# One transpose on TensorE becomes two half-width matmuls, a copy on ScalarE goes, and four masks change engine

## The chip, the cores and the metric

One core of one Trainium2 chip. The metric is the device time of one execution in microseconds. The engines are named as in the profile: PE is TensorE's matmuls and PEld its weight loads, DVE is VectorE, ACT is ScalarE, POOL is GpSimd, SP is SyncE, which here only issues transfers. The kernel before takes 735.45 us (median of 3 runs, 735.43 to 735.67).

## The reference

Attention that keeps only the 32 largest scores of a row, then a gated sum of four two-layer networks (experts), then a layer with the largest of three products:

```
scores = (q @ k^T) / sqrt(64)            # 2 batches, 8 heads, 576 rows, 64 wide, fp32
kth    = 32nd largest score of the row
attn   = exp(scores - max) where scores >= kth, else 0
attn   = attn / (sum(attn) + 1e-9)
x      = attn @ v                        # heads side by side: 1152 x 512
p      = domain_probs / (sum + 1e-9)
out    = sum over e of p[:, e] * (relu(x @ w1[e]) @ w2[e])     # 4 experts, 512 -> 1024 -> 512
h      = max(out @ m1, out @ m2, out @ m3)                     # 512 -> 768
return h @ m_out                                               # 1152 x 512
```

## The kernel before

**Pairs.** The 1152 rows are nine tiles of 128. For attention the heads go two by two, so there are 36 pairs (one tile, two heads), numbered 0 to 35. The tile in the middle (MIXED) holds rows of both batches. Pairs 0 to 3 are tile 0, 4 to 7 tile 1 and so on; 16 to 23 alternate between tiles 4 and 5. Pairs 17, 24, 28 and 32 are the first pairs of tiles 5 to 8: their scores are made early in the kernel, stored to DRAM and loaded back (`later_scores`).

**What a pair does.** `scores` multiplies q and k on PE (pss), ACT copies the result out (s). `topk` finds the 32 largest on DVE in seven steps of eight. `negate` and `exp` prepare and make p = exp(s - max) on ACT. `mask` sets p to zero where s is under the 32nd value and sums it. There are three ways: on DVE in one instruction (line 541), on POOL (lines 544, 545, 549), or on ACT (lines 534 to 536), where no separate exp is made: a Prelu that is steep on one side, a small bias and an Exp with the sum. `ON_ACT` says which pairs do the first and the second head on ACT. `trans_p` transposes p on PE (psp) in pieces of 128 columns, ACT copies them out (pt). `pv` multiplies with v on PE (psv): one full-width matmul (line 601), then eight matmuls (line 604) that alternate between the output partitions 0 to 63 (first head) and 64 to 127 (second head).

**The reciprocal row.** psv holds the unnormalised result with head dimensions on the partitions and the tile's rows along the columns, so the sums, which stand one per partition, must be laid along the columns. `guard` adds 1e-9 on ACT, `recip` makes rr, 128 x 2, on DVE, `spread` copies each of the two numbers to 64 columns on ACT (rb, line 582), `trans_r` transposes that on PE (psr, line 587), ACT copies it out (r, line 589). `norm` multiplies psv by r on DVE, `split_x` makes a high part on ACT and a low part on POOL.

**Products.** Experts and the last layer multiply in three passes of high and low parts: lines 764 to 766. The weights are loaded by SP, rounded to a high part by ACT (whi, line 269), and the low part is the difference, made by POOL or DVE (wlo, line 275).

**Order.** All engines execute in the order in which the program is written. The function `attention` runs over slots, eight per pair, and puts each step of a pair into a slot by a table of numbers (`FIRST`, `MIDDLE`, `TIGHT`, `SECOND`, `THIRD`, `BOTH`, `LOOSE`). A pair whose second head is masked on ACT takes `BOTH`, one masked on DVE takes `LOOSE` (for the later pairs). After each slot, product work is placed until its planned PE time (`clock["pe"]`) has caught up with the planned DVE time (`clock["dve"]`). So the numbers of the table and the DVE work that a step declares set how attention and products alternate on PE. The conversion of the last layer's weights (`to_float32`) starts at slot 306.

Of the kernel before, what the change touches and what calls it, by code (L numbers as in the profile page):

```python
# [10 lines left out]
F32 = mybir.dt.float32  # L11
# [3 lines left out]
AF = mybir.ActivationFunctionType  # L15
# [16 lines left out]
ON_POOL = ((0, 1), (0, 1, 4))  # L32
W_AHEAD = 4
WIDE, W_FROM, W_STEP = 4, 306, 2
ON_ACT = (range(2, 36), (2, 5, 6, 8, 9, 10, 12, 13, 14))
STEEP = 2.0 ** 100
MASK_LATE = 2

FIRST = dict(stag=2, new=1, scores=-12, trans=11, pv=17, rec=16, lag=2, sum=4, late=1)
MIDDLE = dict(stag=2, new=1, scores=-12, at=(11, 12), pv=14, rec=12, lag=1, sum=0, late=1)  # L40
TIGHT = dict(stag=3, new=1, scores=-7, at=(10, 11), guard=11, rec=11, spread=12, pv=12, turn=12, norm=13, split=13, last=14, lag=0, lag_s=1, sum=0, late=1)
SECOND = dict(TIGHT, norm=14, split=14, last=15)
THIRD = dict(stag=4, new=1, scores=-4, at=(11, 12), guard=12, rec=13, spread=13, pv=14, turn=14, norm=15, split=15, last=16, lag=0, lag_s=2, sum=0)
BOTH = dict(stag=4, new=1, scores=-4, at=(14, 14), pv=17, rec=15, lag=2, lag_t=1, sum=0, late=1)
LOOSE = dict(stag=4, new=1, scores=-4, at=(14, 14), pv=17, rec=15, split=22, last=24, lag=2, sum=0)

# [15 lines left out]
def kernel(  # L62
# [14 lines left out]
    nc = tc.nc  # L77
    B, HP, D, _, S = k.shape
    NT, DM = out.shape
    E = gates.shape[2]  # L80
    P = 128
# [13 lines left out]
    def batches(t):  # L95
        return (0, 1) if t == MIXED else (0 if t < MIXED else 1,)
# [16 lines left out]
    at = ctx.enter_context(tc.tile_pool(name="at", bufs=2))  # L113
# [7 lines left out]
    ident = const.tile([P, P], F32, name="ident")  # L121
# [12 lines left out]
    def pe(n):  # L134
        clock["pe"] += n / 2400.0

    def bank(name):
        return pg.tile([P, 512], F32, tag="g", name=name)
# [306 lines left out]
    class Pair:  # L445
        def __init__(self, n):
# [8 lines left out]
            self.on_pool = [n in ON_POOL[j] for j in range(2)]  # L455
            self.on_act = [n in ON_ACT[j] for j in range(2)]

# [119 lines left out]
            dve(60)  # L577
            nc.vector.reciprocal(out=self.rr, in_=self.rs)

        def spread(self):  # L580
            self.rb = at.tile([P, 2, D], F32, tag="rb", bufs=1, name="rb")
            nc.scalar.activation(out=self.rb, in_=self.rr.unsqueeze(2).to_broadcast([P, 2, D]), func=AF.Copy)

        def trans_r(self):
            ps = bank("psr")
            pe(260)
            nc.tensor.transpose(ps[:, 0:P], self.rb.rearrange("p a d -> p (a d)"), ident)
            self.r = at.tile([P, P], F32, tag="r", name="r")
            return lambda: [nc.scalar.activation(out=self.r, in_=ps[:, 0:P], func=AF.Copy), self.did.add("r")]

# [36 lines left out]
    def attention():  # L627

        NP = len(pairs)
        prs = {}  # L630
        later, between = {}, {}

        def options(n):
            return TIGHT if n == HP - 1 else SECOND if n == 2 * HP - 1 else MIDDLE if n in (HP - 2, 2 * HP - 3, 2 * HP - 2) else FIRST if n < 2 * HP else THIRD if n == 3 * HP - 1 else BOTH if n in ON_ACT[1] else LOOSE

        def at_slot(s, f, *a):
            later.setdefault(s, []).append((f, a))


        first_use = {}  # L640
        for n, (c, hp, t) in enumerate(pairs):
            for b in batches(t):
                if ("v", b, hp) not in first_use:
                    first_use["v", b, hp] = n
                    at_slot(8 * n + (options(n)["pv"] - 7 if b and hp else 0), load_v, b, hp)
                if t >= FULL:
                    first_use.setdefault(("k", b, hp), n)
            if t >= FULL and (t, hp) not in later_scores:
                first_use.setdefault(("q", c, hp), n)
            elif n and t < FULL:  # L650
                o = options(max(0, n - 2))
                at_slot(max(8 * n + options(n)["scores"] - LOAD_FULL, 8 * (n - 2) + o["scores"] + o["stag"] + 1), load_full, n)
        free = {"k": -99, "q": -99}
        for key, n in first_use.items():
            if key[0] == "v":
                continue
            s0 = 8 * n
            load, split = (load_k, split_k) if key[0] == "k" else (load_q, split_q)
            at = max(s0 + options(n)["scores"] - (SPLIT_K if key[0] == "k" else SPLIT_Q), free[key[0]] + 2)
            if key[0] == "k" and key[1] and key[2]:  # L660

                at = max(at, 8 * pairs.index((MIXED, key[2] - 1, MIXED)) + options(n)["scores"] + options(n)["stag"] + (1 if key[2] == HP - 1 else 4))
            at_slot(max(at - LOAD, free[key[0]] + 1), load, *key[1:])
            at_slot(at, split, *key[1:])
            free[key[0]] = at
        for n, (c, hp, t) in enumerate(pairs):
            s0 = 8 * n
            prs[n] = Pair(n)
            pr = prs[n]
            o = options(n)  # L670

            def two(s, f, *a, lag=o["lag"]):
                at_slot(s, lambda: at_slot(s + lag, f(*a)))
            for j in range(2):
                b0 = s0 + o["stag"] * j
                two(b0 + o["scores"] - SOONER * ((t, hp) in later_scores), pr.scores, j, lag=o.get("lag_s", o["lag"]))
                for i in range(7):
                    if o["new"]:
                        later.setdefault(b0 + i, []).insert(0, (pr.topk, (j, i)))
                    else:  # L680
                        at_slot(b0 + i, pr.topk, j, i)
                at_slot(b0 + 2, pr.negate, j)
                at_slot(b0 + 5, pr.exp, j)
                late = o.get("late", MASK_LATE) * pr.on_act[j]
                two(b0 + 7 + late, pr.mask, j, lag=o["sum"] if n < EARLY else 3)
                two(s0 + o["at"][j] if "at" in o else b0 + o["trans"] + late + (late > 0), pr.trans_p, j, lag=o.get("lag_t", o["lag"]))
            two(s0 + o["at"][1] if "at" in o else s0 + o["stag"] + o["trans"], pr.trans_p, 2, lag=o.get("lag_t", o["lag"]))
            at_slot(s0 + o.get("guard", o["rec"] - 1), pr.guard)
            at_slot(s0 + o["rec"], pr.recip)
            if o is LOOSE:  # L690
                at_slot(s0 + o["rec"], at_slot, s0 + o["rec"] + 1, pr.spread)
            else:
                at_slot(s0 + o.get("spread", o["rec"] + 1), pr.spread)
            at_slot(s0 + o["pv"], pr.pv)
            two(s0 + o.get("turn", o["rec"] + 2), pr.trans_r)
            end = max(o["pv"], o["rec"] + 2) + o["lag"]
            if n == 1:
                at_slot(s0, nc.sync.dma_start, gate, gates)
            if n == HP - 1:
                between.setdefault(s0 + o["norm"], []).append((norm_gates, ()))  # L700
            if "norm" in o:
                between.setdefault(s0 + o["norm"], []).append((pr.norm, ()))
            else:
                at_slot(s0 + end + 1, pr.norm)
            two(s0 + o.get("split", end + 2), pr.split_x)
        at_slot(-5, load_soon)
        two(9, two_soon, 0, lag=1)
        two(13, two_soon, 1, lag=3)
        for i, t in enumerate((7, *SOON_TWO, 6)):
            at_slot(17 + 3 * i, store_soon, t)  # L710
        last = {}
        for n, p in enumerate(pairs):
            o = options(n)
            last[p[0:2]] = 8 * n + o.get("last", max(o["pv"], o["rec"] + 2) + 2 * o["lag"] + 2)
        for n in range(len(alone)):
            at_slot(ALONE_FROM + ALONE_STEP * n, load_alone, n + 1)
        end = max(last.values()) + 1
        s = min(later)
        while s <= end:
            todo = later.pop(s, [])  # L720
            i = 0
            while i < len(todo):
                f, a = todo[i]
                f(*a)
                todo[i + 1:i + 1] = between.pop(s, [])
                todo += later.pop(s, [])
                i += 1
            if s > 8 * NP + 2:
                clock["dve"] += PAUSE
            yield s, [c for c in last if last[c] + (READY if c[1] == HP - 2 else 0) == s]  # L730
            s += 1

        while narrowed[0] < WIDE * len(wide):
            clock["dve"] += PAUSE
            yield s, []
            s += 1


    lag = []
# [435 lines left out]
```

## Time and profile before

| | before |
|---|---|
| median of 3 runs | 735.45 us |
| profiled execution | 734.86 us |
| its span, first to last instruction | 733.0 us |
| PE busy | 715.2 us (98%) |
| PEld busy | 637.1 us (87%) |
| DVE busy | 580.2 us (79%) |
| ACT busy | 504.8 us (69%) |
| POOL busy | 476.7 us (65%) |

Times in rows are microseconds from the span's start unless they are durations. A PE record lasts longer than it holds the engine, since the next one starts while it drains; what a matmul costs is the distance from its start to the next start. Attention ends near 446 us; products run from about 34 us to the end. The timeline merges equal instructions that follow each other into one row with a count.

### The profile page before, as it was taken

The numbers are of one execution on the slowest core, as the hardware profiler recorded it, in microseconds if no ns is written. First come the engines' busy times: TensorE is split into PE (matmuls) and PEld (weight loads), VectorE is DVE, ScalarE is ACT, GpSimd is POOL, SyncE is SP. The second block draws the span as 40 slices with busy tenths as digits, with TensorE's granted clock in tenths as the row PEclk, the third lists the DMA queues.
The fourth block names the chain that finished last, engine by engine and source line by source line (L and its number), as shares of the span: only waits on it lengthen the run. The fifth ranks groups of instructions, "written<-read, shape, count | busy, mean of one in ns | idle before, by whom it ended". The sixth has DMA issues, their size and how long they took to land. (4 is left out here: it accounts for less than half of the span.)

```text
span 733.0 us, 13786 instructions
## 1 busy us (share of the span) xinstructions
PE 715.2 (98%) x4758; PEld 637.1 (87%) x4758; DVE 580.2 (79%) x1174; ACT 504.8 (69%) x1127; POOL 476.7 (65%) x416
## 2 busy tenths in 40 slices
PE   5899999999999999999999999999999999999997
PEld 3687679889999998899988998999889998998996
DVE  7999989989999999999999974766879873323441
ACT  4868889899987886788888876556566753442431
POOL 2514779678989975879779867856745773532520
PEclk9999999999999999999999999999999999999999
DMA  8995555635756553555455436786879855543501
GB/s 238 303 281 203 146 180 156 181 113 165 208 154 197 150 164 111 170 170 177 137 165 173 139 122 216 267 299 209 294 238 338 256 189 211 167 147 114 188 1 43
DMA packets 57813, 135.26 MB, mean 185 GB/s; under 512 B 9936, under 2 KB 23120, under 8 KB 57744
## 3 DMA queue, kind: packets, MB, share of 16 engines
q1 hardware_dynamic: 49248, 125.74, 54.7%
q10 hardware_dynamic: 8496, 8.65, 3.4%
q8 instruction: 37, 0.61, 0.3%
q14 instruction: 32, 0.26, 0.1%
HBM read 123.36 MB, written 11.01 MB: 183 GB/s over the span
## 5 line engine op out<-in xcount | busy, mean ns | idle before, releaser
L275 POOL TENSOR_TENSOR wlo<-raw,whi 128x512 fp32r<-128x512 f32 x252 | 332.0, 1347 | 135.1 <-ACT whi L269 124.8
L269 ACT ACTIVATE whi<-raw 128x1024 fp32r<-128x1024 f32 x164 | 169.9, 1058 | 18.6 <-PE ps L766 10.2
L764 PE MATMUL ps<-xl,whi 128*128 128x256 f32 (+1 forms) x584 | 173.6, 297 | 0.5 <-POOL xl L625 0.5
L766 PE MATMUL ps<-xh,wlo 128*128 128x256 f32 (+1 forms) x584 | 170.7, 292 | 0.0
L765 PE MATMUL ps<-xh,whi 128*128 128x256 f32 (+1 forms) x584 | 170.6, 292 | 0.0
L513 DVE MAX8 m<-work 128x8 f32<-128x576 f32 x216 | 155.1, 744 | 0.1
L764 PEld LDWEIGHTS ps<-xl,whi 128*128 128x128 f32 x584 | 110.8, 190 | 1.6 <-POOL xl L625 0.7
L765 PEld LDWEIGHTS ps<-xh,whi 128*128 128x128 f32 x584 | 109.7, 188 | 0.9 <-issue 0.2
L766 PEld LDWEIGHTS ps<-xh,wlo 128*128 128x128 f32 x584 | 109.7, 188 | 0.0
L515 DVE MATCH_REPLACE8 work<-m,work 128x576 f32<-128x576 f32 x144 | 106.6, 741 | 0.0
L275 DVE TENSOR_TENSOR wlo<-raw,whi 128x1024 fp32r<-128x1024 f32 x38 | 54.7, 1445 | 49.7 <-ACT whi L269 36.8
L764 PE MATMUL ps<-wlo,h 128*128 128x512 f32 x224 | 91.0, 406 | 2.1 <-POOL wlo L275 1.9
L766 PE MATMUL ps<-whi,h 128*128 128x512 f32 x224 | 87.8, 392 | 0.0
L765 PE MATMUL ps<-whi,h 128*128 128x512 f32 x224 | 87.6, 391 | 0.0
L245 POOL TENSOR_TENSOR narrow<-narrow,raw 128x256 int32<-128x256 int32 x48 | 46.5, 976 | 21.3 <-DMA narrow<-narrow 5.7
L513 DVE MAX8 m<-s 128x8 f32<-128x576 f32 x71 | 53.1, 747 | 2.5 <-ACT s L495 2.5
L495 ACT ACTIVATE s<-pss 128x288 f32<-128x288 f32 x128 | 45.5, 401 | 12.0 <-PE pss L475 7.1
L515 DVE MATCH_REPLACE8 work<-m,s 128x576 f32<-128x576 f32 x72 | 53.3, 741 | 0.0
L764 PEld LDWEIGHTS ps<-wlo,h 128*128 128x128 f32 x224 | 42.8, 191 | 11.3 <-POOL wlo L275 5.0
L562 ACT ACTIVATE pt<-psp 128x512 f32<-128x512 f32 x72 | 40.0, 600 | 15.7 <-PE psp L559 15.6
L766 PEld LDWEIGHTS ps<-whi,h 128*128 128x128 f32 x224 | 42.1, 188 | 9.9 <-POOL h L904 0.5
L1042 DVE TENSOR_TENSOR tm<-ps,tm 128x384 f32<-128x384 f32 x36 | 19.8, 556 | 39.0 <-PE ps L766 39.0
(118 smaller groups left out, 1493.7 us busy)
## 6 DMA issues: line engine op xcount, KB each, us to landing
raw<-in_w_dram SPq DMA_DIRECT2D x128, 512.0 KB, 4.3
raw<-narrow SPq DMA_DIRECT2D x36, 512.0 KB, 4.5
raw<-in_m_dram SPq DMA_DIRECT2D x36, 256.0 KB, 5.1
whole<-in_w_dram SPq DMA_DIRECT2D x14, 512.0 KB, 5.5
narrow<-narrow ACTq DMA_DIRECT2D x48, 128.0 KB, 5.0
kraw<-in_k_dram SPq DMA_DIRECT2D x16, 288.0 KB, 4.5
raw<-in_mo_dram SPq DMA_DIRECT2D x12, 256.0 KB, 5.8
kfull<-in_k_dram SPq DMA_DIRECT2D x9, 288.0 KB, 5.2
```

The source lines that it names most:

```text
L245: nc.gpsimd.tensor_tensor(out=out.bitcast(I32), in0=out.bitcast(I32), in1=last, op=ALU.add)
L269: nc.scalar.activation(out=hi, in_=raw, func=AF.Copy)
L275: on.tensor_tensor(out=lo[:, x], in0=raw[:, x], in1=hi[:, x].bitcast(F32), op=ALU.subtract)
L495: nc.scalar.activation(out=s[:, h, :], in_=halves[h][:, 0:SH], func=AF.Copy)
L513: nc.vector.max(m[:, 8 * r:8 * r + 8], src)
L515: nc.vector.match_replace(out=self.w[j], in_to_replace=m[:, 8 * r:8 * r + 8], in_values=src, imm_value=NEG)
L562: return lambda: [nc.scalar.activation(out=d, in_=ps.rearrange("p (r n) -> p r n", r=NR), func=AF.Copy), self.did.add(("pt", part))]
L764: nc.tensor.matmul(ps, lhsT=lh, rhs=rl, start=first, stop=False)
L765: nc.tensor.matmul(ps, lhsT=lh, rhs=rh, start=False, stop=False)
L766: nc.tensor.matmul(ps, lhsT=ll, rhs=rh, start=False, stop=last)
L1042: nc.vector.tensor_tensor(out=tm[:, g], in0=ps, in1=tm[:, g], op=ALU.max)
```

## The change

`spread` goes with its tile rb. `trans_r` makes psr with two matmuls: the weights are one column of rr, read as 64 equal columns, the moving side is the identity, the output 64 partitions each. `trans_r` now stands in the slot of `pv` for all pairs. The pairs 17, 24, 28 and 32 enter the second list of `ON_ACT`, and with it take the table `BOTH` in place of `LOOSE`.

```
-ON_ACT = (range(2, 36), (2, 5, 6, 8, 9, 10, 12, 13, 14))
+ON_ACT = (range(2, 36), (2, 5, 6, 8, 9, 10, 12, 13, 14, 17, 24, 28, 32))
...
-TIGHT = dict(stag=3, new=1, scores=-7, at=(10, 11), guard=11, rec=11, spread=12, pv=12, turn=12, norm=13, split=13, last=14, lag=0, lag_s=1, sum=0, late=1)
+TIGHT = dict(stag=3, new=1, scores=-7, at=(10, 11), guard=11, rec=11, pv=12, norm=13, split=13, last=14, lag=0, lag_s=1, sum=0, late=1)
...
-        def spread(self):
-            self.rb = at.tile([P, 2, D], F32, tag="rb", bufs=1, name="rb")
-            nc.scalar.activation(out=self.rb, in_=self.rr.unsqueeze(2).to_broadcast([P, 2, D]), func=AF.Copy)
-
         def trans_r(self):
             ps = bank("psr")
             pe(260)
-            nc.tensor.transpose(ps[:, 0:P], self.rb.rearrange("p a d -> p (a d)"), ident)
+            for j in range(2):
+                nc.tensor.matmul(ps[j * D:(j + 1) * D, 0:P], lhsT=self.rr[:, j:j + 1].to_broadcast([P, D]), rhs=ident, start=True, stop=True)
...
-            if o is LOOSE:
-                at_slot(s0 + o["rec"], at_slot, s0 + o["rec"] + 1, pr.spread)
-            else:
-                at_slot(s0 + o.get("spread", o["rec"] + 1), pr.spread)
             at_slot(s0 + o["pv"], pr.pv)
-            two(s0 + o.get("turn", o["rec"] + 2), pr.trans_r)
+            two(s0 + o["pv"], pr.trans_r)
```

On PE, at the first pair (its psv, and the pss of later pairs behind it), the rows before:

```order
L601 MATMUL psv<-pt_303,v_last_112 128x128
L604 MATMUL psv<-pt,vt 64x128 x8
L475 MATMUL pss<-kfull,qfull 128x288
L348 MATMUL pss<-kfull,qraw 128x288
L475 MATMUL pss<-kfull,qfull 128x288
L348 MATMUL pss<-kfull,qraw 128x288
L587 MATMUL psr<-ident,rb 128x128
L559 MATMUL psp<-ident,p 128x128 x4
```

and after (line numbers are smaller by 3 or 7 in the new file):

```order
L598 MATMUL psv<-pt_303,v_last_112 128x128
L601 MATMUL psv<-pt,vt 64x128 x8
L584 MATMUL psr<-ident,rr 64x128 x2
L475 MATMUL pss<-kfull,qfull 128x288
L348 MATMUL pss<-kfull,qraw 128x288
L475 MATMUL pss<-kfull,qfull 128x288
L348 MATMUL pss<-kfull,qraw 128x288
L559 MATMUL psp<-ident,p 128x128 x4
```

Here psr has moved ahead of four pss; the fifth pair moves in the same way. At the ninth pair, as in all the rest, psr stood directly behind psv before and still does, with the products behind it. Before:

```order
L601 MATMUL psv<-pt_1442,v_last_112 128x128
L604 MATMUL psv<-pt,vt 64x128 x8
L587 MATMUL psr<-ident,rb 128x128
L764 MATMUL ps_1469<-xl,whi 128x256
L765 MATMUL ps_1469<-xh,whi 128x256
```

and after:

```order
L598 MATMUL psv<-pt_1434,v_last_112 128x128
L601 MATMUL psv<-pt,vt 64x128 x8
L584 MATMUL psr<-ident,rr 64x128 x2
L757 MATMUL ps_1461<-xl,whi 128x256
L758 MATMUL ps_1461<-xh,whi 128x256
```

Nothing else moved there: one row of one instruction is one of two.

On ACT, around the second head of pair 17 (its 32 largest values are m_2812 before and m_2796 after), before:

```order
L495 ACTIVATE s<-pss 128x288 x2
L562 ACTIVATE pt<-psp 128x512 x2
L567 ACTIVATE pt_2856<-psp 128x128
L582 ACTIVATE rb<-rr 128x128
L534 ACTIVATE s<-s,m_2701 128x576
L535 ACTIVATE nb<-m_2701,nb 128x1
L536 ACTIVATE p,rs<-s,nb 128x576
L527 ACTIVATE p<-s,nb 128x576
L413 ACTIVATE qh<-qraw 128x512
L520 ACTIVATE nb<-m_2872 128x1
L495 ACTIVATE s<-pss 128x288 x2
```

and after:

```order
L562 ACTIVATE pt<-psp 128x512 x2
L567 ACTIVATE pt_2840<-psp 128x128
L413 ACTIVATE qh<-qraw 128x512
L520 ACTIVATE nb<-m_2856 128x1
L495 ACTIVATE s<-pss 128x288 x2
L895 ACTIVATE raw<-ps_2729 128x512
L269 ACTIVATE whi<-raw 128x1024 x2
L586 ACTIVATE r<-psr 128x128
L387 ACTIVATE kT<-kraw 128x576 x2
L534 ACTIVATE s<-s,m_2796 128x576
L535 ACTIVATE nb<-m_2796,nb 128x1
L536 ACTIVATE p,rs<-s,nb 128x576
```

The spread (rb) and the exp of line 527 are gone, and the three instructions of the second head's mask stand some ten instructions later, behind the rounding of weights and of k. The mask of the first head (m_2701) stands ahead of the copies pt in the new order. In PE's whole list no matmul is added or lost but for psr; about the four pairs, groups of products and of scores stand somewhat earlier or later.

## Rows read from the trace of the kernel before

**Rows 1.** The page: busy us, share and count by engine; granted clock in slices.

```profile
PE 715.2 (98%) x4758; PEld 637.1 (87%) x4758; DVE 580.2 (79%) x1174; ACT 504.8 (69%) x1127; POOL 476.7 (65%) x416
...
PEclk9999999999999999999999999999999999999999
```

**Rows 2.** Busy us by stretch: length, PE, PEld, DVE, ACT, POOL, clock, DMA, GB/s.

```profile
80.00:446.00 366.00, 362.05 (x2767) 324.29 (x2766) 343.07 (x732) 303.72 (x719) 299.85 (x261) 1.00 0.53 161
446.00:629.00 183.00, 182.78 (x1028) 167.89 (x1027) 127.76 (x230) 105.35 (x196) 112.55 (x97) 1.00 0.73 247
629.00:733.00 104.00, 100.32 (x549) 95.44 (x547) 34.94 (x47) 38.00 (x53) 35.91 (x24) 1.00 0.33 109
```

**Rows 3.** What PE's matmuls waited for: us in total, times, longest.

```profile
PE ps L764 <- POOL wlo L275: 1.9, 5, 0.8
...
PE psp L559 <- ACT p L536: 0.3, 1, 0.3
```

**Rows 4.** Groups by line and shape: count, busy us, mean ns, idle before.

```profile
L534 ACT ACTIVATE s<-s,m 128x576 f32<-128x576 f32 x43 | 33.4, 777 | 0.3 <-DVE m L513 0.3
L536 ACT ACTIVATE p<-s,nb 128x576 f32<-128x576 f32 x43 | 33.4, 777 | 1.4
...
L527 ACT ACTIVATE p<-s,nb 128x576 f32<-128x576 f32 x29 | 22.2, 764 | 0.0
...
L535 ACT ACTIVATE nb<-m,nb 128x1 f32<-128x1 f32 x43 | 12.6, 293 | 0.0
L582 ACT ACTIVATE rb<-rr 128x128 f32<-128x128 f32 x36 | 11.5, 318 | 7.4 <-DVE rr L578 7.3
...
L541 DVE SCALAR_TENSOR_TENSOR p<-s,m,p 128x576 f32<-128x576 f32 x24 | 27.3, 1136 | 5.4 <-ACT p L527 5.4
```

**Rows 5.** What PE's weight loads waited for, same columns as rows 3.

```profile
PEld psp L559 <- ACT p L536: 1.4, 2, 1.1
...
PEld psr L587 <- ACT rb L582: 0.5, 2, 0.3
```

**Rows 6.** Timeline of PE near 47 us: start, length, instruction, count.

```profile
46.78 1.17 PE L850 MATMUL psa<-xfull,whole 128*128 128x128 f32 x9
47.78 0.60 PE L559 MATMUL psp<-ident,p 128*128 128x128 f32 x4
48.22 0.61 PE L850 MATMUL psa<-xfull,whole 128*128 128x128 f32 x4
```

**Rows 7.** Timeline of PE at the ninth pair, two windows, and psv's group.

```profile
115.71 1.09 PE L604 MATMUL psv<-pt,vt 128*64 128x128 f32 x16
116.74 0.33 PE L587 MATMUL psr<-ident,rb 128*128 128x128 f32 x1
...
115.98 0.83 PE L604 MATMUL psv<-pt,vt 128*64 128x128 f32 x12
...
L604 PE MATMUL psv<-pt,vt 128*64 128x128 f32 x512 | 35.0, 279 | 0.0
```

**Rows 8.** Timeline of PE at the fifth and at the third pair.

```profile
68.34 1.09 PE L604 MATMUL psv<-pt,vt 128*64 128x128 f32 x16
69.37 1.24 PE L475 MATMUL pss<-kfull,qfull 64*128 64x288 f32 x4
...
43.58 0.33 PE L587 MATMUL psr<-ident,rb 128*128 128x128 f32 x1
43.84 1.23 PE L475 MATMUL pss<-kfull,qfull 64*128 64x288 f32 x4
```

**Rows 9.** POOL's longest wait, and the timeline of PE around a hole.

```profile
POOL wlo L275 <- ACT whi L269: 124.8, 40, 10.7
...
103.41 0.39 PE L765 MATMUL ps<-whi,h 128*128 128x512 f32 x1
103.64 0.40 PE L766 MATMUL ps<-whi,h 128*128 128x512 f32 x1
104.31 0.50 PE L764 MATMUL ps<-wlo,h 128*128 128x512 f32 x1 [0.28 <-POOL wlo L275]
```

More of the change, by code (lines that the diff above doesn't have):

```diff
@@ L40 @@
 MIDDLE = dict(stag=2, new=1, scores=-12, at=(11, 12), pv=14, rec=12, lag=1, sum=0, late=1)
-TIGHT = dict(stag=3, new=1, scores=-7, at=(10, 11), guard=11, rec=11, spread=12, pv=12, turn=12, norm=13, split=13, last=14, lag=0, lag_s=1, sum=0, late=1)
+TIGHT = dict(stag=3, new=1, scores=-7, at=(10, 11), guard=11, rec=11, pv=12, norm=13, split=13, last=14, lag=0, lag_s=1, sum=0, late=1)
 SECOND = dict(TIGHT, norm=14, split=14, last=15)
-THIRD = dict(stag=4, new=1, scores=-4, at=(11, 12), guard=12, rec=13, spread=13, pv=14, turn=14, norm=15, split=15, last=16, lag=0, lag_s=2, sum=0)
+THIRD = dict(stag=4, new=1, scores=-4, at=(11, 12), guard=12, rec=13, pv=14, norm=15, split=15, last=16, lag=0, lag_s=2, sum=0)
 BOTH = dict(stag=4, new=1, scores=-4, at=(14, 14), pv=17, rec=15, lag=2, lag_t=1, sum=0, late=1)
```

## Prediction

> **What bounds the kernel now.** I read the page first: TensorE (PE) holds matmul records for 715.2 of 733.0 us, 98%, and its granted clock is at full speed in all slices [rows 1]. A busy PE need not be a limiting PE, so the busy times by stretch come next [rows 2]: from 80 us to the end of attention near 446 us PE is busy for 362.05 of 366 us, so it is without work for only 3.95 us. From 446 to 629 us it lacks 0.22 us, and what it lacks after 629 us (3.7 us) is mostly the last output. VectorE (DVE) is close behind in attention (343.07 of 366), ScalarE (ACT) and GpSimd (POOL) are 17 and 18% free there. In the list of what PE waited for, last, the entries behind the weights' low halves and behind a masked p come to 1.9 and 0.3 us [rows 3]. The conclusion is the frame for all that follows: PE executes a fixed list in a fixed order with hardly a hole, so the time moves by what the list gets longer or shorter, plus what is won from or lost in holes. An engine beside PE that gets lighter pays only through the holes.
>
> **The path of the reciprocal row.** Before, per pair: reciprocal on DVE, spread to 128 columns on ACT (rb), one transpose on PE (psr), copy on ACT (r). After: reciprocal, two plain matmuls of 64 output partitions each against the identity, copy. 36 pairs.
>
> What goes from ACT: 36 spreads of 318 ns, 11.5 us, and up to 7.4 us in which ACT stood idle in front of one, mostly for the reciprocal [rows 4]. PE waited for the spread nearly nowhere: the spread is named in 0.5 us of psr's waits of the weight load, which runs beside the matmuls [rows 5]. So the shorter chain is worth 0.5 us at most directly, and nothing at least.
>
> What comes to PE: the price is read from distances between starts, since a record's own duration overlaps its neighbours. A transpose of 128 columns holds PE for 0.11 us: four start at 47.78 and the next work at 48.22 [rows 6]. A plain fp32 matmul of 128 columns over the whole array stands in the trace as two records at 0.11 us each: nine records from 46.78 to 47.78. So two plain matmuls one after the other would be four records, 0.44 us. But they use the two halves of the array's columns, as the psv matmuls of line 604 do. There the eight matmuls are 16 records in 1.09 us, and the last twelve of them 0.83 us from 115.98 on; less one record's own length (their mean is 0.28) these twelve start within 0.55 us, in five steps of two records, 0.11 us a step [rows 7]. One after the other, 16 records would take 1.7 us. So two records, one of each half, run together, and the new pair of matmuls costs two steps, 0.22 us, against 0.11 us: +0.11 us. The weights have one odd feature, one number per partition read 64 times, that no row shows. The bounds per pair are thus +0.0 us (all four records together: the sum does not change) and +0.33 us (no two together: 36 x 0.33 = 11.8 us). I take +0.11, since the psv rows have the same form (128 rows by 64 columns, 128 moving columns, fp32) and stand right in front of the new ones.
>
> Then the switch between forms. The last psv records start at 115.98 + 0.55 = 116.53 and psr at 116.74 [rows 7]; this step, out of the column halves, is 0.2 rather than 0.11 us. Leaving the halves costs the same when a 64-row matmul follows: from the first psv record to pss it is 68.34 to 69.37, 1.03 us, as from 115.71 to 116.74 here [rows 7, 8]. Today that 0.1 us stands between psv and psr; after, the new psr is of psv's form, and the switch comes behind it. It is moved, not removed. Two pairs win a little: where psr is followed by pss of line 475 it costs 0.26 us to the next start (43.58 to 43.84) [rows 8], a second switch into row halves; after, there is one switch, so these two stand at 1.03 + 0.22 = 1.25 instead of 1.03 + 0.26 = 1.29, about -0.05. In two early pairs (the first and the fifth) psr also moves one slot ahead, next to psv; there the switch between pss and the transposes stays, so I count them as all others. Sum on PE: 34 x 0.11 - 2 x 0.05 = 3.6 us. Nothing covers this: PE is the engine with 3.95 us of holes in 366, and the matmuls are in its list at places where it does not wait.
>
> The Trainium skill, "TensorEngine Tiling (Array Packing)", section Key Properties, says that different tiles can run in parallel and that changing the tiling mode drains TensorE. Both sentences agree with the rows: the pairs of psv records, and the 0.1 us on leaving the halves. By the second alone the change would look good, a switch saved per pair; the order shows that psv's own switch remains behind the new matmuls, so it saves none in 34 pairs of 36.
>
> **The four masks.** The pairs 17, 24, 28 and 32 lose their second head's mask on DVE (1136 ns, 4 x 1.14 = 4.5 us) and on ACT the exp (764 ns), and get on ACT 777 + 293 + 777 = 1847 ns, so 4 x 1.08 = 4.3 us more [rows 4]; the short read of the sum behind each, on both engines, is left out. All this is beside PE. ACT ends up lighter in all: -11.5 + 4.3 = -7.2 us. The pairs also take the settings of the other pairs whose two masks are on ACT (lag 1 on the transposes, the split a slot sooner). The planner counts 4 x 0.67 = 2.7 us less DVE work, so it puts that much less product work between attention steps: PE's list keeps all its matmuls, and those move behind attention, where PE is full too. The cost is nothing at either end as work; as waits it lies between minus a share of the holes and the price of a later p, which the rivals hold. In the trace the 43 masks already on ACT make PE wait 0.3 us in all, and its weight load 1.4 us [rows 3, 5].
>
> **The sum.** PE +3.6 us. From the holes I take back the 0.5 us above. +3.1 us on the profiled execution, 734.86 us (span 733.0 and 1.9 around it), gives 738.0. The median of the runs is 735.45, 0.59 above that execution, so the forecast is 735.45 + 3.1 = 738.5 us.
>
> **Rivals.** What a measurement can tell from no change is about 0.2%, 1.5 us.
>
> 1. Faster: ACT's relief ends PE's waits behind the low halves of the weights. The place is PE's line 764 on wlo, which POOL makes from ACT's whi: POOL waited 124.8 us for whi [rows 9]. One such hole: starts 0.23 us apart, then 103.64 to 104.31, so 0.44 us lost where the row shows 0.28 of idle [rows 9]. By that ratio the 3.95 us of holes cost 3.95 x 0.44 / 0.28 = 6.2 us. If all went, 3.6 - 6.2 = -2.6: 732.9 us. It is faster by the bound once 5.1 of 6.2 us are won, while PE names wlo for 1.9 us of its waits at most and the transposed or masked p for others [rows 3]. For it: ACT is lighter by 7.2 us of work and loses up to 7.4 us of idle time in front of the spreads. Against: four pairs put blocks of 1.8 us on ACT, the very thing that stands ahead of whi. 9%.
>
> 2. No measurable difference: a third to four fifths of these 6.2 us are won, or the added PE time falls into holes whose releaser does not follow PE. 735.45 + 3.6 - 3.1 = about 736. 17%.
>
> 3. The two halves do not run together, because the weights are read with a step of zero or two matmuls are too few to overlap: +11.8 us, 747. Against: eight psv matmuls overlap from the first record on. 5%. The Trainium skill, "TensorE: Matmul & The Clock Gate", section Terms, says that transposes have a mode four times faster for FP32; by it one plain matmul would be 4 x 0.11 = 0.44 us, so two in parallel give the same +0.33 and 747 us. The trace has two records against one for the same columns, a factor of two, so I do not raise the chance.
>
> 4. The mask on ACT becomes a wait of PE: p is ready up to 1.85 us after its turn in four pairs, 7.4 us at full exposure, half of it likely if at all: 738.5 + 3.7 = 742.2. Against: the nine pairs that already have both masks there. 8%.
>
> **How the numbers follow.** Forecast +3.1 with its own range +1.5 to +6 (one more hole per block of ACT masks at 0.4 to 0.9 us, or more holes filled): 61%. Faster is rival 1 alone, 0.09; same is rival 2, 0.17; slower is the forecast with rivals 3 and 4, 0.74. The range takes in the forecast and all of rival 2 (down to 735.0) and the lower half of rival 4 (to 742.0); it leaves out rivals 1 and 3 and the rest.
>
> **What would show it.** In the changed profile psr should be 144 records in 36 groups, in steps of two records 0.11 us apart, with psv to the next product start 0.11 us longer; PE's busy time near 719 us; ACT's near 498 (504.8 - 7.2); DVE's near 576 (580.2 - 4.5); PE's holes from 80 us to the end of attention 3 to 5 us. If the four records come one by one, rival 3 is right; if PE's holes fall under 1 us, rival 1; if psp waits for p on ACT at the four pairs, rival 4. The prediction is wrong if psr costs PE no more than the transpose did, or if the time falls while psr costs what I say: then holes were worth more than the trace of before shows.

## The result, and the profile after

The changed kernel takes 739.83 us (median of 6 runs, 739.47 to 740.71) against 735.56 us before on the same chip: ratio 1.0055, 95% interval 1.0042 to 1.0068, so 3.1 to 5.0 us slower (4.05 by the ratio, 4.3 by the medians). The forecast was 738.5 us, +3.1 us.

One thing is needed to read the numbers of single runs. In the profiled execution the granted clock of PE stood at its lower level, 1.2 GHz, from 26.0 to 29.5 us, after PE had been idle 2.0 us for a pt (before: idle 2.1 us at the same place, the clock stayed at 2.4 GHz). PE's timeline there (start, length, instruction, count, idle before it and its releaser):

```profile
26.21 0.79 PE L598 MATMUL psv<-pt,v_last 128*128 128x128 f32 x2 [2.03 <-ACT pt L567]
26.93 1.98 PE L601 MATMUL psv<-pt,vt 128*64 128x128 f32 x16
```

The first psv took 1.98 us instead of 1.09, and the span is 738.4 us instead of 737.4 to 737.7 in the four runs without it. Below, times are compared from the sixth pair on (psr at 76.10 before, 77.23 after): from there to the end it is 656.9 us before and 661.2 us after, +4.3 us.

Page of the changed kernel, busy time by engine, and its busy times by stretch (length, PE, PEld, DVE, ACT, POOL, clock, DMA, GB/s):

```profile
PE 721.3 (98%) x4866; PEld 644.3 (87%) x4866; DVE 578.8 (78%) x1166; ACT 500.1 (68%) x1103; POOL 474.4 (64%) x416
```

```profile
80.00:446.00 366.00, 362.64 (x2827) 326.01 (x2827) 340.38 (x724) 300.37 (x699) 294.16 (x258) 1.00 0.52 158
446.00:629.00 183.00, 182.16 (x1038) 167.38 (x1035) 129.88 (x231) 105.49 (x197) 116.02 (x101) 1.00 0.76 252
```

PE has 108 more records (4866 for 4758): 144 of psr for 36. DVE is lighter by 1.4 us and ACT by 4.7 [rows 1], where the forecast counted 4.5 and 7.2: the four masks took 4.2 us off DVE, but its 38 differences wlo lasted 1495 ns each for 1445, and of the 2.5 us by which ACT differs the short reads of the sums, left out of the count, make 0.7. PE's idle time is 3.36 us up to 446 us and 0.84 us up to 629 us, 4.20 in all, against 3.95 + 0.22 = 4.17 us [rows 2]. So the holes up to 629 us have the same idle time, and the loss stands in the list.

The ninth pair, PE's timeline after, which answers to [rows 7]:

```profile
116.85 1.09 PE L601 MATMUL psv<-pt,vt 128*64 128x128 f32 x16
117.78 0.39 PE L584 MATMUL psr<-ident,rr 128*64 128x128 f32 x4
118.09 0.39 PE L757 MATMUL ps<-xl,whi 128*128 128x256 f32 x1
118.32 0.28 PE L758 MATMUL ps<-xh,whi 128*128 128x256 f32 x1
```

Four records of psr in 0.39 us, two steps, right behind the psv records with no switch between: 0.93 us from the first psv record, not 1.03 [rows 7]. Then come 0.31 us from the first record of psr to the first product and another 0.23 to the second, which in a run of products stands 0.12 behind the first. Before, psr to the first product was 0.08 and on to the second 0.20. From the first psv record to the second product it is 1.47 us, before 1.31 (115.71 to 117.02): +0.16, where the forecast had +0.11. From the record ahead of psv to the second product it is 0.15 to 0.17 us more at the other late pairs too, where PE does not wait and the neighbours are the same kind of work.

What PE waited for, after (total, times, longest):

```profile
PE psv L598 <- ACT pt L567: 4.1, 5, 2.0
...
PE ps L757 <- POOL wlo L275: 1.0, 4, 0.3
PE ps L757 <- DVE h L904: 0.8, 1, 0.8
```

and before, for pt:

```profile
PE psv L601 <- ACT pt L567: 3.1, 3, 2.1
```

The waits behind wlo fell from 1.9 us [rows 3] to 1.0. The three waits for pt that were there before (near 26, 94 and 144 us) are still there and two have come, near 298 and 399 us; the wait for h is new. PE's rows at the longer of the two and at h:

```profile
297.56 0.29 PE L483 MATMUL pss<-kT,qh 128*128 128x288 f32 x1
298.64 0.49 PE L598 MATMUL psv<-pt,v_last 128*128 128x128 f32 x2 [0.78 <-ACT pt L567]
...
469.75 0.34 PE L759 MATMUL ps<-xh,wlo 128*128 128x384 f32 x1
470.93 0.41 PE L757 MATMUL ps<-xl,whi 128*128 128x384 f32 x1 [0.84 <-DVE h L904]
```

### The profile page after: what moved, and what is told of

Same layout as the page of the kernel before. It is cut to its first block, busy times and chain, and to the rows that moved or that the text cites. A ratio compares the mean times of both kernels' runs of the same rounds, so it can differ in the third digit from the quotient of the medians.

```text
span 738.4 us, 13987 instructions
## 1 busy us (share of the span) xinstructions
PE 721.3 (98%) x4866; PEld 644.3 (87%) x4866; DVE 578.8 (78%) x1166; ACT 500.1 (68%) x1103; POOL 474.4 (64%) x416
## 5 line engine op out<-in xcount | busy, mean ns | idle before, releaser
L275 DVE TENSOR_TENSOR wlo<-raw,whi 128x1024 fp32r<-128x1024 f32 x38 | 56.6, 1495 | 56.3 <-ACT whi L269 43.8
```

What stands on the lines that cost most here:

```text
L275: on.tensor_tensor(out=lo[:, x], in0=raw[:, x], in1=hi[:, x].bitcast(F32), op=ALU.subtract)
```

## The experiments

Ten kernels ran in three groups, each group on one chip beside runs of the kernel before (medians 735.27 to 735.88); the ratios are against those. The changed kernel itself ran in none of the groups, so where a kernel is set against it the two times come from different groups.

**1. The reciprocal row alone.**

```
-ON_ACT = (range(2, 36), (2, 5, 6, 8, 9, 10, 12, 13, 14, 17, 24, 28, 32))
+ON_ACT = (range(2, 36), (2, 5, 6, 8, 9, 10, 12, 13, 14))
```

> The new reciprocal row alone (no spread, two half-width matmuls); the masks stay where they were before. Theory A: the matmuls are the whole loss. From the changed kernel's trace, behind the half-width records the next product starts 203 ns later and the one behind that 226 ns later, so a pair costs 0.158 us more on PE than before, about 4.9 us over all pairs; with 0.5 us taken back from holes about 739.9 us, the same as the changed kernel's 739.8 within 1 us. Rival B: the masks carry the loss through new waits (psv for pt, and the product at 470 us); then this kernel is near 736 to 737.

Measured: 740.6 us (739.08 to 741.53), ratio 1.0046 (1.0022 to 1.0070). It is as slow as the whole change: theory A. From the sixth pair to the end its trace is 5.35 us longer than before. Two of PE's waits have come or grown, for h (none before) and for wlo at pso (0.2 us before):

```profile
PE psp L564 <- DVE h L904: 1.6, 1, 1.6
...
PE pso L757 <- DVE wlo L275: 1.2, 1, 1.2
```

**2. The masks alone**, the same line edited in the kernel before.

> The four masks on ScalarE alone; spread and transpose as before. Theory A: 735.5 within 0.7 us, since only VectorE and ScalarE change. Rival B (the masks carry the loss): 738 to 739.5.

Measured: 739.17 us (737.62 to 739.99), ratio 1.0031 (1.0013 to 1.0049). Theory A falls here: the masks are not free. They lose 2.3 us alone by the ratio (3.3 by the medians, 3.05 from the sixth pair on in the traces), the row alone 3.4 (4.7, 5.35) and the whole change 4.05 (4.3, 4.3), so the two parts don't add up. PE's own list is that of the kernel before but for the order; its idle time from 80 to 446 us is 6.6 us (359.40 busy) for 3.95. PE's waits, and its timeline at the largest hole:

```profile
PE psv L601 <- ACT pt L567: 5.3, 5, 1.9
```

```profile
296.45 0.29 PE L483 MATMUL pss<-kT,qh 128*128 128x288 f32 x1
298.29 0.49 PE L601 MATMUL psv<-pt,v_last 128*128 128x128 f32 x2 [1.55 <-ACT pt L567]
```

and ACT there:

```profile
293.44 0.60 ACT L909 ACTIVATE h<-ps 128x512 fp32r<-128x512 f32 x1
295.24 0.78 ACT L534 ACTIVATE s<-s,m 128x576 f32<-128x576 f32 x1 [1.20 <-DVE m L513]
295.93 0.28 ACT L535 ACTIVATE nb<-m,nb 128x1 f32<-128x1 f32 x1
296.24 0.78 ACT L536 ACTIVATE p<-s,nb 128x576 f32<-128x576 f32 x1
296.92 0.19 ACT L536 ACTIVATION_READ_ACCUMULATOR p<-s,nb 128x1 f32 x1
297.01 1.06 ACT L562 ACTIVATE pt<-psp 128x512 f32<-128x512 f32 x2
297.97 0.28 ACT L567 ACTIVATE pt<-psp 128x128 f32<-128x128 f32 x1
```

ACT stands idle 1.20 us for the 32nd value, does a mask, and only then the three copies pt. This is not the mask that moved to ACT but one that was on ACT before; in the new order it stands ahead of pt.

**3. ScalarE relieved, by a wide reciprocal on VectorE** (in the kernel before, `spread` left empty).

```
-            nc.vector.reciprocal(out=self.rr, in_=self.rs)
+            nc.vector.reciprocal(out=self.rb, in_=self.rs.unsqueeze(2).to_broadcast([P, 2, D]))
```

> The kernel before without the spread on ScalarE: the reciprocal on VectorE reads each sum 64 times and writes the 128 columns itself, the transpose stays. It takes the 11.5 us from ScalarE as the change does, adds about 0.12 us per pair to VectorE and nothing to PE. Theory A (ScalarE's relief pays only through PE's holes): 735.0, between 734.3 and 735.6. Rival C (the relief is worth some us and the matmuls ate it): 731 to 733.5.

Measured: 748.3 us (748.06 to 748.95), ratio 1.0153 (1.0123 to 1.0183). Neither theory: the experiment failed by its own cost. VectorE's group of the reciprocal:

```profile
L578 DVE RECIPROCAL rb<-rs 128x128 f32<-128x128 f32 x36 | 33.8, 939 | 0.5 <-ACT rs L572 0.5
```

939 ns, not the 0.27 assumed: 28 us more on VectorE, which is then busy for 360.64 of 366 us, and PE waits at many places.

**4. Which matmul stands behind the switch** (in the changed kernel; psr also goes ahead of psv).

```
-                nc.tensor.matmul(ps[:, cols], lhsT=last, rhs=self.pt[2][:, cols], start=True, stop=False)
                 for r in range(NR):
...
+                nc.tensor.matmul(ps[:, cols], lhsT=last, rhs=self.pt[2][:, cols], start=False, stop=True)
```

> The changed kernel with PE's order turned within psv: psr first, then the eight half-width psv matmuls, then the full-width one of the tail, so that a full-width fp32 matmul and not a product stands behind the switch out of the column halves. Same matmuls in number and size. Theory A: the mis-sized 0.05 us per pair is the switch meeting the product's weights; it goes, 36 x 0.05 = 1.8 to 2 us: 737.8. Rival D (the cost lies in the halves' own steps or anywhere in the switch, wherever it stands): 739.8 within 0.7.

Measured: 738.72 us (738.35 to 741.09), ratio 1.0034 (1.0013 to 1.0055): 1.1 us under the changed kernel by the medians, between the theories; the intervals overlap, so the total decides nothing. The timeline does:

```profile
115.23 0.29 PE L483 MATMUL pss<-kT,qh 128*128 128x288 f32 x1
115.45 0.44 PE L584 MATMUL psr<-ident,rr 128*64 128x128 f32 x4
115.72 1.04 PE L600 MATMUL psv<-pt,vt 128*64 128x128 f32 x16
116.70 0.49 PE L602 MATMUL psv<-pt,v_last 128*128 128x128 f32 x2
116.94 0.36 PE L757 MATMUL ps<-xl,whi 128*128 128x256 f32 x1
117.14 0.28 PE L758 MATMUL ps<-xh,whi 128*128 128x256 f32 x1
```

From the last pss to the second product: 1.91 us. In the changed kernel, from a pss at 116.41 to 118.32: 1.91. Before, 115.27 to 117.02: 1.75. The pair's price did not move, so the switch costs the same before a product and before a plain fp32 matmul (D). What this kernel won came from holes: from the record ahead of the pair to the second one behind it, it takes 2.33 us for 2.92 near 94 us, 2.51 for 2.96 near 297 us and 2.03 for 2.47 near 398 us, all places where psv waits for pt in the changed kernel.

**5. psr twice** (in the changed kernel).

```
-            for j in range(2):
+            for j in (0, 1, 0, 1):
```

> The changed kernel with the two half-width matmuls of psr issued twice (the second two write the same values again). Theory A (PE is the bound and a step of two half-width records costs 0.109 us, as between the new records): 36 x 0.218 = +7.8 us over the changed kernel, 747.4; somewhat less if holes take some of it, at least 746. Rival E (PE has slack in attention that hides added matmuls): under 743.5.

Measured: 747.91 us (747.33 to 749.16), ratio 1.0163 (1.0135 to 1.0190): +8.1 us over the changed kernel, theory A. At the ninth pair:

```profile
118.69 1.09 PE L601 MATMUL psv<-pt,vt 128*64 128x128 f32 x16
119.61 0.61 PE L584 MATMUL psr<-ident,rr 128*64 128x128 f32 x8
120.15 0.38 PE L757 MATMUL ps<-xl,whi 128*128 128x256 f32 x1
120.37 0.28 PE L758 MATMUL ps<-xh,whi 128*128 128x256 f32 x1
```

From psv to the second product 1.68 us, 0.21 more than with two matmuls: 36 x 0.21 = 7.6 us of the 8.1. Work added to PE's list reaches the end in full.

**6. The masks with the old table** (in the kernel with the masks alone).

```
-            return TIGHT if n == HP - 1 else SECOND if n == 2 * HP - 1 else MIDDLE if n in (HP - 2, 2 * HP - 3, 2 * HP - 2) else FIRST if n < 2 * HP else THIRD if n == 3 * HP - 1 else BOTH if n in ON_ACT[1] else LOOSE
+            return TIGHT if n == HP - 1 else SECOND if n == 2 * HP - 1 else MIDDLE if n in (HP - 2, 2 * HP - 3, 2 * HP - 2) else FIRST if n < 2 * HP else THIRD if n == 3 * HP - 1 else BOTH if n in ON_ACT[1] and n < 16 else LOOSE
```

> The four masks on ScalarE alone, as in the run of the masks before, but the four pairs keep the table of the pairs masked on VectorE (LOOSE instead of BOTH). On ScalarE the copies pt then stand ahead of the neighbour's mask again, as in the kernel before. Theory F: the masks' loss of some 3 us is this order: PE's psv waits for a pt that stands behind a mask which waits for VectorE. Then the holes of 1.7 and 1.0 us at psv go and the time is 736 within 0.7. Rival G: the 4.3 us of work on ScalarE, or the planner's smaller product share, is the loss: 738 to 739, like the masks alone.

Measured: 735.52 us (735.09 to 742.30), ratio 1.0002 (0.9976 to 1.0028). Theory F: the same four masks on ACT, the loss gone. ACT and PE at the same place as in the second experiment:

```profile
293.14 0.60 ACT L909 ACTIVATE h<-ps 128x512 fp32r<-128x512 f32 x1
293.62 1.09 ACT L562 ACTIVATE pt<-psp 128x512 f32<-128x512 f32 x2
294.57 0.31 ACT L567 ACTIVATE pt<-psp 128x128 f32<-128x128 f32 x1
295.73 0.31 ACT L582 ACTIVATE rb<-rr 128x128 f32<-128x128 f32 x1 [0.85 <-DVE rr L578]
```

```profile
296.10 0.29 PE L483 MATMUL pss<-kT,qh 128*128 128x288 f32 x1
296.24 0.38 PE L601 MATMUL psv<-pt,v_last 128*128 128x128 f32 x2
```

The copies pt come first, and psv follows pss at once.

**7. The whole change with the old table** (the same edit in the changed kernel).

> The changed kernel, but the four pairs keep LOOSE instead of BOTH. Theory F: the two psv holes of 0.95 and 0.35 us go, so 738.5 to 739.3. Rival G: the same as the changed kernel, 739.8 within 0.5.

Measured: 738.67 us (737.91 to 739.87), ratio 1.0032 (1.0011 to 1.0054), in the range of theory F. Both psv holes are gone from its trace; the 1.0 us one near 468 us stays. So the table costs about 1.2 us in the change by the medians (1.5 from the sixth pair on in the traces; the intervals of the two kernels overlap), where PE is later at psv anyway, and more when the masks move alone.

**8 and 9. ScalarE relieved, by GpSimd and by VectorE** (in the kernel before).

```
-            nc.scalar.activation(out=self.rb, in_=self.rr.unsqueeze(2).to_broadcast([P, 2, D]), func=AF.Copy)
+            nc.gpsimd.tensor_copy(out=self.rb, in_=self.rr.unsqueeze(2).to_broadcast([P, 2, D]))
```

and with `nc.vector.tensor_copy`.

> The kernel before with the spread made by GpSimd instead of ScalarE; transpose and masks as before. ScalarE is relieved of 11.5 us and of the idle time in front, PE has no added work, GpSimd gets 36 copies of about 0.46 us. Theory A (ScalarE's relief pays only through PE's holes): 735.2 between 734.3 and 736. Rival C (the relief is worth some us): 731 to 733.5. If GpSimd's queue delays the transposes, psr waits for rb show it, and the time is over 737.

> The kernel before with the spread made by a copy on VectorE right behind its own point in the order, instead of on ScalarE; transpose and masks as before. ScalarE is relieved as in the change; VectorE, 94% busy in attention, gets 36 copies of some 0.2 to 0.3 us (its 128x128 product takes 0.27), 7 to 10 us. Theory A (VectorE's added work shows only where it makes holes on PE): 735.5 to 738.5. Rival C (ScalarE's relief is worth some us by itself): 731 to 734.

Measured: GpSimd 768.91 us (768.45 to 774.57), ratio 1.0456 (1.0422 to 1.0491); VectorE 739.36 us (738.88 to 739.79), ratio 1.0053 (1.0039 to 1.0068). With GpSimd PE waits in psr:

```profile
PE psr L587 <- POOL rb L582: 26.4, 12, 6.3
```

The copy itself is short (0.29 us) but queues behind GpSimd's other work, mostly the weights' low halves. The granted clock also stood at 1.2 GHz for 17 us in four stretches between 124 and 254 us, each near a wait of PE of 2.2 to 6.3 us, so the 33 us over the kernel before are not all waiting. With VectorE, ACT is lighter by 7.1 us from 80 to 446 us (296.63 for 303.72), yet DVE rises to 356.77 of 366 us and PE's idle time to 7.45 us. Rival C, a gain from a lighter ScalarE, showed in none of the three runs; but each loaded another engine, so a free relief was not measured and this stays open.

Why the copies on VectorE took 18.6 us and not 7 to 10 stands in the rows of both engines. One copy, and GpSimd beside it:

```profile
225.93 1.23 DVE L582 COPY rb<-rr 128x128 f32<-128x128 f32 x1
...
224.25 2.83 POOL L388 TENSOR_TENSOR kT<-kraw,kT 64x576 fp32r<-64x576 f32 x2
227.16 3.79 POOL L275 TENSOR_TENSOR wlo<-raw,whi 128x512 fp32r<-128x512 f32 x3
```

The copy ends 0.08 us after the GpSimd instruction that was running when it started. Of 36 copies, the 11 that started with GpSimd idle took 196 to 227 ns; of the other 25, 24 ended 82 to 89 ns after the GpSimd instruction beside them did.

**10. Toward a kernel under both** (in the sixth kernel).

```
-WIDE, W_FROM, W_STEP = 4, 306, 2
+WIDE, W_FROM, W_STEP = 4, 308, 2
```

> The kernel before with the four masks on ScalarE, the table LOOSE kept for these pairs, and the conversion of the last layer's weights begun two slots later (308 for 306). The one hole left against the kernel before, 1.0 us at 465 us, is a product that waits for VectorE's h, which stands behind a conversion. Theory H: later conversions free VectorE there, the hole goes and the time is 734.5 within 0.7, so at best 0.1 to 0.2% under the kernel before. Rival J: the hole or another one comes back elsewhere, above all where the conversion ends near 617 us: 735.5 to 737.5.

Measured: 734.71 us (733.60 to 739.29), ratio 0.9994 (0.9978 to 1.0010). PE lacks nothing from 446 to 629 us in its trace, so the hole went as theory H says; its gain over the kernel before cannot be told from none.

```profile
446.00:629.00 183.00, 183.00 (x1030) 168.42 (x1029) 128.42 (x229) 105.29 (x195) 110.38 (x98) 1.00 0.75 249
```

## Why the prediction was right, and where it was off

**The frame was right.** PE executes a list with few holes, and what is added to the list is added to the time: doubling psr gave 8.1 us for 7.6 counted, and the row alone was as slow as the whole.

**The price of psr: right in kind, small by a third.** The forecast's step "the new pair of matmuls costs two steps, 0.22 us, against 0.11 us: +0.11 us" is exact for the steps: 144 records, psr 0.93 us behind the first psv and two steps of 0.11. "It is moved, not removed" is where it was mis-sized: the forecast took the 0.1 us up to the next start for the whole switch. Leaving the halves costs 0.2 us in all (0.31 - 0.22 = 0.09 to the first product, 0.23 - 0.12 = 0.11 more to the second). Before, it cost 0.15: 0.10 ahead of psr, and 0.05 behind it, since psr to the second product took 0.28 where 0.11 + 0.12 would do. The transpose behind the halves had hidden the other 0.05. The 0.20 from the first product to the second is by itself no mark of the switch; before, it stands behind transposes with no halves near as well, where the two steps together are 0.23:

```profile
111.93 0.27 PE L564 MATMUL psp<-ident,p 128*128 128x128 f32 x1
111.96 0.36 PE L764 MATMUL ps<-xl,whi 128*128 128x256 f32 x1
112.16 0.28 PE L765 MATMUL ps<-xh,whi 128*128 128x256 f32 x1
```

The fourth kernel shows that the cost is not that of a product behind the switch: a plain fp32 matmul there changed nothing. So a pair costs 0.16. Why a transpose hides a part, no run shows. The two pairs before a 64-row pss were right: psv to pss took 1.24 us (43.76 to 45.00) where 1.25 was worked out:

```profile
43.76 1.09 PE L601 MATMUL psv<-pt,vt 128*64 128x128 f32 x16
...
45.00 0.51 PE L475 MATMUL pss<-kfull,qfull 64*128 64x288 f32 x1
```

With 0.16 for 0.11 the forecast's sum over 36 pairs becomes 5.3 us, not 3.6; the 31 pairs from the sixth on come to 5.0.

**The holes: right in sum by luck, wrong in parts.** The forecast took 0.5 us back, for PE's waits behind the spread. Counting holes by distances between starts over the usual ones, those of 0.15 us and more after 80 us cost 6.2 us before and 5.7 us after. 5.0 - 0.5 = 4.5, near the 4.3 us from the sixth pair on. But what went (the hole at 289.9 us, one at 147 us) and what came (psv at 298 and 399 us, 0.95 and 0.35; a product at 470 us, 1.0) are different things. The forecast put the four masks at nothing as work and left their waits to the rivals, and the section on the change had said where this fails: on ACT the first head's mask stands ahead of the copies pt in the new order. It priced the instructions that move and not the one that another table put in front of a copy that PE needs. Nor did it name psv's wait for pt, with 3.1 us the largest of PE's waits for another engine in the trace of before. Rival 4 had a wait of about this size in view, 3.7 us, but the wrong one: psv waits for pt, not psp for p.

**The parts don't add.** From the sixth pair on, 5.35 us for the row alone and 3.05 for the masks alone make 8.4, the change has 4.3 (by the ratios 5.7 against 4.05). PE, which is later in the change, waits less for pt (1.7 us lost near 298 us in the masks alone, 0.95 in the change), and the first kernel's waits of psp for h and of pso for wlo are not in the change's list. The second is in accord with DVE being lighter by the masks, but no run isolated it; why the parts do not add stays open beyond these two.

**Rival 1** (ACT's relief wins the holes behind wlo) had a core: PE's waits there fell by 0.9 us. It was far from 5.1. **Rival 2** is out by the interval, **rival 3** by the records: two together, 0.11 us a step.

## What to carry to other kernels

Where one engine has no holes, price every instruction by the distance between starts, and price the switch of array form by the whole stretch up to the second instruction behind it: the step that was hidden by a neighbour comes out when the neighbour goes. Moving work between engines that wait on each other in order is priced by what then stands in front of what; read the new order for copies that the bound engine needs and that now stand behind an instruction with a late input. Test a table apart from the work that it moves: here the four masks alone were free and the table was not.

## What was not expected of the hardware

A reciprocal on VectorE of 128 x 128 numbers took 939 ns and of 128 x 2 numbers 153 ns, about 6 ns for each further column, while a product of 128 x 128 takes 272 ns. A copy of 128 x 128 on VectorE that reads two numbers 64 times took 196 to 1228 ns, median 465: about 0.2 us with GpSimd idle, else until just after the GpSimd instruction beside it ended (24 of 25). The wide reciprocal, in a kernel with the same work on GpSimd, stayed within 930 to 952 ns. Weights read with a step of zero load like others: 137 ns in the median and steps of 0.11 us for psr, as for psv.
